# Cutting the last output tile in two and reordering the end-of-kernel waits in a fused attention-and-GEGLU kernel

## The chip, the cores and the metric

The kernel runs on one core of a Trainium2 chip (trn2). The metric is device time in microseconds (us), the median over runs of one kernel; a run's time is about 2 us longer than the span that its profile shows. The granted clock (the share of TensorE's full clock that its throttle let through) was 0.996 to 1.0. Engines in the profile: PE is TensorE's matmuls, PEld its weight loads, DVE is VectorE, ACT is ScalarE, POOL is GpSimd, SP is the sequencer that issues every DMA of this kernel ("SPq" is that sequencer).

## The reference

One normalised input feeds two branches, and both are added to the input. S is 2048 tokens, D is 512.

```python
xn = layernorm(x)                                   # [1, 2048, 512]
# A: 32 heads of 16, each token attends to 8 keys, at distances 0, 2, ..., 14
q, k, v = split(xn @ wqkv)
a = softmax(q . k[idx] * scale, masked where idx < 0) @ v[idx]
# B: GEGLU, hidden size 1376
h = gelu(xn @ w_gate) * (xn @ w_up)
out = x + a @ wo + h @ w_down
```

## The kernel before

The kernel is written as a graph of tasks (matmul groups, evictions, transfers). A list scheduler with a cost model orders them on each engine when the kernel is built; the chip then runs each engine's list in order, with semaphore waits where a task depends on another engine. The tokens are done in four blocks of 512. The last stage of a block makes four output tiles of 128 tokens: 11 matmuls with `Wd` (the down projection of B) and 4 with `Wo` (the output projection of A) accumulate in one bank of PSUM (the memory that matmuls write to), DVE adds the input rows `XR` and writes bf16 to `OB` (this is called the eviction of the bank), and SP stores `OB`:

```python
for ti in range(4):
    t = 4 * b + ti                       # t = 15 is the last tile of the kernel
    it_acc = Item("acc%d" % t, P_ps, "acc")
    it_ob = Item("ob%d" % t, P_ob, "ob") # two OB buffers
    # PE, task "acc": 11 x (HT_j x Wd_j), then 4 x (OT_dq x Wo_dq), all of 512 columns
    # DVE, task "fin":
    e.tensor_tensor(out=OB[:, ito.slot, :], in0=PS[:, 512*it.slot:512*it.slot+512],
                    in1=XR[:, itx.slot, :], op=ALU.add)
    # SP, task "sto":
    e.dma_start(out2[128*t:128*t+128, :], OB[:, it.slot, :])
    ...
```

Transfers rotate over 24 semaphores. When SP has issued the last transfer, the code lets it wait for the final value of each of them, in the order in which they were made:

```python
if eng_name == "sp":
    for (s, tot) in self.dma_totals:
        e.wait_ge(s, tot)
```

## Time and profile before

| | before |
|---|---|
| time, median of the first 3 runs | 214.04 us (213.99 to 214.37) |
| span in the profile | 212.0 us |
| PE busy | 203.9 us, 96% |
| end of the last matmul | 208.3 us |
| end of the last DVE instruction | 209.08 us |
| last store landed | 210.80 us |
| end of the span | 212.0 us |

From the page of the kernel before: the span, then each engine's busy time (share of the span, number of instructions), then the engines' shares of the chain that ended last. (26 records of matmuls are missing: the weight loads, one for each matmul, number 1548 here.)

```profile
span 212.0 us, 3824 instructions
PE 203.9 (96%) x1522; PEld 101.0 (48%) x1548; DVE 147.9 (70%) x237; ACT 115.2 (54%) x190; POOL 12.8 (6%) x44
PE 86%; DVE 7%; issue 2%; ACT 2%; DMA 1%; POOL 0%; ACTq 0%; DVEq 0%; POOLq 0%
```

The body of the kernel is one stream on PE. The end is not. These are lines of the timeline of the kernel before, for the last 8 us (start, duration, engine, line of the kernel, operation, what it writes and reads, count; in brackets the idle time before it and what ended that):

```profile
204.85 2.54 PE L1268 MATMUL PS<-Wd,HT 128*128 128x512 bf16 x11
205.87 3.57 SPq L1319 DMA_DIRECT2D out_dram<-OB  x2
207.23 1.03 PE L1281 MATMUL PS<-Wo,OT 128*128 128x512 bf16 x4
208.39 0.69 DVE L1313 TENSOR_TENSOR OB<-PS,XR 128x512 bf16<-128x512 f32 x1 [2.55 <-PE PS L1281]
```

The 15 matmuls of tile 15 start 0.216 us apart, the last at 207.88, and end at 208.26. The eviction runs from 208.39 to 209.08. The store is issued behind it (the second of the two that the SPq line merges, at 209.11). How long SP waited for the store is in the waits of the DMA queue (who waited for whom, total us, times, longest), and how long the store took from issue to landing is in the DMA view of the last 5 us (size, median us to landing):

```profile
SPq L512 <- DMA out_dram<-OB: 1.4, 1, 1.4
```

```profile
out_dram<-OB SPq DMA_DIRECT2D x1, 128.0 KB, 1.7
```

The line of the final waits itself, in the view of one source line (count, duration min/median/max in ns, first and last start in us), has its first record at 210.8, when the store has landed, and its last at 211.5:

```profile
L512 SPq EVENT_SEMAPHORE  x12: 17/28/28, 210.8 to 211.5; - x12
```

Which semaphores those records test is in the trace's raw records: start in us, duration in ns, engine, operation, `>=` for a semaphore it waits on. Semaphores 103 to 126 are the kernel's 24, in the order in which they were made, so 115 is place 12 of the list, counted from 0:

```
last landing of a transfer: 210.801
209.109 333 Sync DMA_DIRECT2D      $S[101]>= semaphore=115
210.817  17 Sync EVENT_SEMAPHORE   $S[115]>=
210.875  28 Sync EVENT_SEMAPHORE   $S[116]>= $S[114]>=
210.948  28 Sync EVENT_SEMAPHORE   $S[117]>= $S[113]>=
...
211.495  28 Sync EVENT_SEMAPHORE   $S[126]>= $S[104]>=
211.563  38 Sync COMPARE_BRANCH    $S[103]>=
```

So the 24 waits do not run as they are written. Place 12 runs first and alone, then pairs from the middle outward, and place 0 rides on the branch that leaves the block. The last store was the 133rd transfer, and that is place 12: the first wait blocked until the store had landed, and 0.76 us passed from there to the branch.

### The profile page before, as it was taken

What the parts mean: (1) busy time and instruction counts of PE and PEld (TensorE: products, weight loads), DVE (VectorE), ACT (ScalarE), POOL (GpSimd) and SP (SyncE); (2) the same over time, 40 slices, a digit from 0 to 9 for tenths busy, and PEclk for the clock granted to TensorE, in tenths of its full rate; (3) what the DMA queues carried; (4) which work ended last, traced back from release to release, by engine and by line L of the source; (5) the groups of instructions that cost most, each with busy time, mean ns of one, the idle gap of its engine ahead of it and who ended that gap; (6) DMA issues with size and microseconds to landing.
All of it is one profiled execution on the core that took longest, in us unless ns stands there. A gap on an engine that the chain in (4) does not pass through costs nothing.

```text
span 212.0 us, 3824 instructions
## 1 busy us (share of the span) xinstructions
PE 203.9 (96%) x1522; PEld 101.0 (48%) x1548; DVE 147.9 (70%) x237; ACT 115.2 (54%) x190; POOL 12.8 (6%) x44
## 2 busy tenths in 40 slices
PE   7999999999999999999999999999999999998993
PEld 2445565454444664544444654444445554443440
DVE  4508999999998597599822687697622877796121
ACT  2398667987810169976710259878400459847000
POOL 6701010010013000000000000000000000000000
PEclk9999999999999999999999999999999999999999
DMA  6999969023069610021011359030012258040111
GB/s 170 374 397 360 237 163 245 2 56 98 28 176 237 176 34 0 0 56 48 0 50 52 104 167 223 8 99 3 0 58 90 77 154 220 3 99 0 52 50 49
DMA packets 23489, 23.40 MB, mean 110 GB/s; under 512 B 2640, under 2 KB 22448, under 8 KB 23472
## 3 DMA queue, kind: packets, MB, share of 16 engines
q1 hardware_dynamic: 23472, 23.16, 38.6%
q8 instruction: 12, 0.20, 0.4%
q14 instruction: 5, 0.04, 0.1%
HBM read 18.94 MB, written 4.21 MB: 109 GB/s over the span
## 4 chain that ended last, share of the span: by engine, by line
PE 86%; DVE 7%; issue 2%; ACT 2%; DMA 1%; POOL 0%; ACTq 0%; DVEq 0%; POOLq 0%
PE PS L1229 31%; PE PS L1007 19%; PE PS L1268 18%; PE PS L1281 7%; PE PS L1069 6%; DVE PVS L1183 4%; PE PS L1198 3%; PE PS L965 2%; DVE st L894 1%; DMA XIN<-in_A_x_dram 1%; PE PS L1151 1%; DVE XN L952 1%; ACT PT L1160 1%; ACT xnT L973 0%; DVE HT L1250 0%
## 5 line engine op out<-in xcount | busy, mean ns | idle before, releaser
L1051 DVE TENSOR_TENSOR PROD<-QT,KT 128x2048 bf16<-128x2048 bf16 x32 | 37.3, 1219 | 11.5 <-ACT KT L1025 11.5
L1229 PE MATMUL PS<-xnT,Wu 128*128 128x512 bf16 (+1 forms) x171 | 44.4, 379 | 0.3
L1229 PE MATMUL PS<-xnT,Wg 128*128 128x512 bf16 (+1 forms) x171 | 44.2, 379 | 0.3
L1268 PE MATMUL PS<-Wd,HT 128*128 128x512 bf16 (+1 forms) x171 | 40.2, 379 | 0.4 <-ACT OT L1209 0.2
L1183 DVE TENSOR_TENSOR PVS<-BS,PT 128x2048 bf16<-128x2048 bf16 x32 | 37.0, 1219 | 3.6 <-ACT PT L1160 3.5
L1313 DVE TENSOR_TENSOR OB<-PS,XR 128x512 bf16<-128x512 f32 x16 | 11.0, 689 | 32.4 <-PE PS L1281 32.3
L1238 ACT ACTIVATE GG<-PS 128x512 bf16<-128x512 f32 (+1 forms) x44 | 26.6, 606 | 6.4 <-PE PS L1229 5.9
L1007 PE MATMUL PS<-xnT,Wqkv 128*128 128x512 bf16 x121 | 29.1, 379 | 1.0 <-issue 0.5
L1245 ACT ACTIVATE UU<-PS 128x512 bf16<-128x512 f32 (+1 forms) x44 | 26.6, 605 | 4.6 <-PE PS L1229 4.4
L1032 ACT ACTIVATE VT<-PS 128x512 bf16<-128x512 f32 x16 | 9.6, 598 | 34.4 <-PE PS L1007 34.4
L1268 PEld LDWEIGHTS PS<-Wd,HT 128*128 128x128 bf16 (+1 forms) x176 | 17.1, 98 | 21.0 <-ACT OT L1209 0.6
L1229 PEld LDWEIGHTS PS<-xnT,Wu 128*128 128x128 bf16 (+1 forms) x176 | 16.9, 100 | 18.6 <-ACT QT L1018 0.4
L1229 PEld LDWEIGHTS PS<-xnT,Wg 128*128 128x128 bf16 (+1 forms) x176 | 17.0, 100 | 18.1
L1025 ACT ACTIVATE KT<-PS 128x512 bf16<-128x512 f32 x16 | 9.6, 598 | 18.5 <-PE PS L1007 18.5
L1007 PEld LDWEIGHTS PS<-xnT,Wqkv 128*128 128x128 bf16 x128 | 11.9, 98 | 15.9 <-ACT KT L1025 0.8
L1250 DVE TENSOR_TENSOR HT<-GG,UU 128x512 bf16<-128x512 bf16 (+1 forms) x44 | 16.8, 419 | 2.2 <-ACT UU L1245 2.2
L1069 PEld LDWEIGHTS PS<-E,PROD 128*128 128x128 bf16 x512 | 15.8, 96 | 4.5
L1281 PE MATMUL PS<-Wo,OT 128*128 128x512 bf16 x64 | 16.4, 378 | 0.0
L1069 PE MATMUL PS<-E,PROD 128*128 128x8 bf16 x512 | 15.8, 166 | 0.0
L1007 PE MATMUL PS<-xnT,WV 128*128 128x512 bf16 x60 | 14.9, 378 | 0.3
L894 DVE BATCH_NORM_STATS2 st<-XIN 128x6 f32<-128x512 bf16 x16 | 10.7, 686 | 2.8 <-DMA XIN<-in_A_x_dram 2.8
L973 ACT ACTIVATE xnT<-PS 128x1024 bf16<-128x1024 bf16 x8 | 8.2, 1020 | 6.8 <-PE PS L965 6.8
(57 smaller groups left out, 148.4 us busy)
## 6 DMA issues: line engine op xcount, KB each, us to landing
BS<-vt_scratch SPq DMA_DIRECT2D x64, 128.5 KB, 3.4
XR<-in_A_x_dram SPq DMA_DIRECT2D x16, 128.0 KB, 2.2
vt_scratch<-VT SPq DMA_DIRECT2D x16, 128.0 KB, 1.7
out_dram<-OB SPq DMA_DIRECT2D x16, 128.0 KB, 2.0
XIN<-in_A_x_dram SPq DMA_DIRECT2D x7, 256.0 KB, 3.5
Wg<-in_B_w_gate_dram SPq DMA_DIRECT2D x1, 1376.0 KB, 9.2
Wu<-in_B_w_up_dram SPq DMA_DIRECT2D x1, 1376.0 KB, 12.2
Wd<-in_B_w_down_dram SPq DMA_DIRECT2D x1, 1280.0 KB, 10.3
```

The costliest lines, as they stand in the source:

```text
L894: return lambda e: e.bn_stats(out=st[:, t, :], in_=XIN[:, it.slot, t2, :])
L1007: ins = e.matmul(PS[:, 512 * it.slot:512 * it.slot + HWD], lhsT=lhsT, rhs=xnT[:, kt, c0:c0 + HWD], start=(kt == 0), stop=(kt == 3))
L1051: return lambda e: e.tensor_tensor(out=PROD[:, it.slot, :, :], in0=bass.AP(QT, (itq.slot * 4 + g) * 512, [[NQT * 4 * 512, 128], [0, 4], [1 ...
L1069: ins = e.matmul(PS[:, col:col + 8], lhsT=PROD[:, it.slot, jj, ti * 128:(ti + 1) * 128], rhs=E8[:, :], start=True, stop=True)
L1183: return lambda e: e.tensor_tensor(out=PVS[:, ito.slot, half, :, :], in0=BS[:, it.slot, :, o:o + 512], in1=bass.AP(PT, (itp.slot * 2 + hal ...
L1229: ins = e.matmul(PS[0:M, 512 * it.slot:512 * it.slot + 512], lhsT=Wx[:, kt, j * 128:j * 128 + M], rhs=xnT[:, kt, c0b:c0b + 512], start=(kt ...
L1238: return lambda e: e.activation(out=GG[0:M, ito.slot, :], in_=PS[0:M, 512 * it.slot:512 * it.slot + 512], func=ACTF.Gelu_apprx_tanh)
L1245: return lambda e: e.activation(out=UU[0:M, ito.slot, :], in_=PS[0:M, 512 * it.slot:512 * it.slot + 512], func=ACTF.Identity)
L1250: return lambda e: e.tensor_tensor(out=HT[0:M, ito.slot, j, :], in0=GG[0:M, ig.slot, :], in1=UU[0:M, iu.slot, :], op=ALU.mult)
L1268: ins = e.matmul(PS[:, 512 * it.slot:512 * it.slot + 512], lhsT=HT[0:K, ith.slot, j, ti * 128:(ti + 1) * 128], rhs=Wd[0:K, j, :], start=(j ...
L1281: ins = e.matmul(PS[:, 512 * it.slot:512 * it.slot + 512], lhsT=OT[:, ito.slot, dq, ti * 128:(ti + 1) * 128], rhs=Wo[:, dq, :], start=Fals ...
L1313: return lambda e: e.tensor_tensor(out=OB[:, ito.slot, :], in0=PS[:, 512 * it.slot:512 * it.slot + 512], in1=XR[:, itx.slot, :], op=ALU.add)
```

## The change

Its intent is to shorten what happens after the last matmul. It lists the final waits so that the oldest transfers are tested first and the newest on the branch, and it cuts tile 15 into 384 and 128 columns, each with its own PSUM bank, eviction, output buffer and store. It also generalises the loads of `Wg` and `Wu` to chunks, but the default is one chunk of all 11 column groups, which is the two loads of before.

```diff
         if eng_name == "sp":
-            for (s, tot) in self.dma_totals:
+            newest = {id(t.sem): i for i, t in enumerate(self.order["sp"])}
+            totals = sorted(self.dma_totals, key=lambda x: newest[id(x[0])])
+            n = len(totals)
+            runs_in = [n // 2]
+            for i in range(1, n // 2):
+                runs_in += [n // 2 + i, n // 2 - i]
+            runs_in.append(0)
+            listed = [None] * n
+            for place, x in zip(runs_in, totals):
+                listed[place] = x
+            for (s, tot) in listed:
                 e.wait_ge(s, tot)
...
+    TAIL_SPLIT = cfg.get("TAIL_SPLIT", [15])
...
-                it_acc = Item("acc%d" % t, P_ps, "acc")
-                it_ob = Item("ob%d" % t, P_ob, "ob")
+                cparts = [(0, 384), (384, 512)] if t in TAIL_SPLIT else [(0, 512)]
+                for ci, (c0, c1) in enumerate(cparts):
+                    CW = c1 - c0
+                    it_acc = Item("acc" + sfx, P_ps, "acc")
+                    it_ob = Item("ob" + sfx, P_ob, "ob")
...                  # matmuls with rhs Wd[0:K, j, c0:c1] and Wo[:, dq, c0:c1]
-                    G.task("dve", "fin%d" % t, 0.69, mk_fin(), rd=[it_acc, it_xr], wr=[it_ob], prio=base + 61)
+                        G.task("dve", "fin" + sfx, 0.16 + CW * 1.04e-3, mk_fin(), rd=[it_acc, it_xr], wr=[it_ob],
+                               prio=base + 61)
...
-                    return lambda e: e.dma_start(out2[128 * t:128 * t + 128, :], OB[:, it.slot, :])
+                        return lambda e: e.dma_start(out2[128 * t:128 * t + 128, c0:c1], OB[:, it.slot, 0:CW])
```

More of the change, by code (lines that the diff above doesn't have):

```diff
@@ L659, in bass_parallel_sum__sliding_local_dilated__glu_gated_geglu__prompt_kernel @@
     R_WD = cfg.get("R_WD", 100)
+    R_WG = cfg.get("R_WG", -800)
+    TAIL_SPLIT = cfg.get("TAIL_SPLIT", [15])
     NHALF = cfg.get("NHALF", [1, 1, 1, 1])
@@ L855, in bass_parallel_sum__sliding_local_dilated__glu_gated_geglu__prompt_kernel, with mk @@
                                       prio=13))
-        G.task("sp", "ld_wg", 0, lambda e: e.dma_start(
-            Wg[:, :, :], B_w_gate.rearrange("(k p) n -> p k n", p=128)), wr=[I_wg], prio=-800, nbytes=DF * 1024)
-        G.task("sp", "ld_wu", 0, lambda e: e.dma_start(
-            Wu[:, :, :], B_w_up.rearrange("(k p) n -> p k n", p=128)), wr=[I_wu], prio=-799, nbytes=DF * 1024)
+        WCH = cfg.get("WCHUNK", [11])
+        wch_of = {}
+        j0 = 0
+        for ci, nj in enumerate(WCH):
+            c_lo = j0 * 128
+            c_hi = min(DF, (j0 + nj) * 128)
+            for j in range(j0, j0 + nj):
+                wch_of[j] = ci
+            for (nm, Wx, I_w, src) in (("g", Wg, I_wg, B_w_gate), ("u", Wu, I_wu, B_w_up)):
+                def mk(Wx=Wx, src=src, c_lo=c_lo, c_hi=c_hi):
+                    return lambda e: e.dma_start(
+                        Wx[:, :, c_lo:c_hi], src[:, c_lo:c_hi].rearrange("(k p) n -> p k n", p=128))
+                G.task("sp", "ld_w%s%d" % (nm, ci), 0, mk(), wr=[(I_w, ci)], prio=R_WG + 2 * ci + (nm == "u"),
+                       nbytes=(c_hi - c_lo) * 1024)
+            j0 += nj
         G.task("sp", "ld_wd0", 0, lambda e: e.dma_start(
@@ L1234, in bass_parallel_sum__sliding_local_dilated__glu_gated_geglu__prompt_kernel @@
                     G.task("pe", "f%s%d_%d" % (nm, b, j), d_mm(512, 4), mk_f(),
-                           rd=[(I_xnT, 2 * b), (I_xnT, 2 * b + 1), I_w], wr=[it_p], prio=fb + j, mode="f")
+                           rd=[(I_xnT, 2 * b), (I_xnT, 2 * b + 1), (I_w, wch_of[j])], wr=[it_p], prio=fb + j,
+                           mode="f")
                 def mk_gl(it=it_g, ito=it_gg, M=M):
@@ L1256, in bass_parallel_sum__sliding_local_dilated__glu_gated_geglu__prompt_kernel @@
                 t = 4 * b + ti
-                it_acc = Item("acc%d" % t, P_ps, "acc")
                 it_xr = Item("xr%d" % t, P_xr, "xr")
-                it_ob = Item("ob%d" % t, P_ob, "ob")
-                fin_pe = FIN_PE or (t >= FIN_PE_FROM)
-                def mk_ad(ti=ti, it=it_acc, ith=it_ht, itx=it_xr, fin_pe=fin_pe):
-                    def f(e):
-                        ins = None
-                        for j in range(NJ):
-                            K = 128 if j < 10 else DF - 1280
-                            ins = e.matmul(PS[:, 512 * it.slot:512 * it.slot + 512],
-                                           lhsT=HT[0:K, ith.slot, j, ti * 128:(ti + 1) * 128], rhs=Wd[0:K, j, :],
-                                           start=(j == 0), stop=False)
-                        if fin_pe:
-                            ins = e.matmul(PS[:, 512 * it.slot:512 * it.slot + 512], lhsT=ident[:, :],
-                                           rhs=XR[:, itx.slot, :], start=False, stop=False)
-                        return ins
-                    return f
@@ L1277, in mk_aw @@
-                def mk_aw(ti=ti, it=it_acc, ito=it_ot):
-                    def f(e):
-                        ins = None
-                        for dq in range(4):
-                            ins = e.matmul(PS[:, 512 * it.slot:512 * it.slot + 512],
-                                           lhsT=OT[:, ito.slot, dq, ti * 128:(ti + 1) * 128], rhs=Wo[:, dq, :],
-                                           start=False, stop=(dq == 3))
-                        return ins
-                    return f
@@ L1286, in bass_parallel_sum__sliding_local_dilated__glu_gated_geglu__prompt_kernel @@
-                rd_d = [it_ht, I_wd] + ([it_xr, I_ident] if fin_pe else [])
-                if ACC_SPLIT:
-                    G.task("pe", "accd%d" % t, d_mm(512, 12 if fin_pe else 11), mk_ad(), rd=rd_d, wr=[it_acc],
-                           prio=base + R_ACCD, mode="f")
-                    G.task("pe", "accw%d" % t, d_mm(512, 4), mk_aw(), rd=[it_ot, I_wo, it_acc], wr=[it_acc],
-                           prio=base + 60, mode="f")
-                else:
-                    def mk_a(fd=mk_ad(), fw=mk_aw()):
-                        def f(e):
-                            fd(e)
-                            return fw(e)
-                        return f
-                    G.task("pe", "acc%d" % t, d_mm(512, 16 if fin_pe else 15), mk_a(),
-                           rd=rd_d + [it_ot, I_wo], wr=[it_acc], prio=base + 60, mode="f")
@@ L1303, in bass_parallel_sum__sliding_local_dilated__glu_gated_geglu__prompt_kernel @@
                 G.task("sp", "ldxr%d" % t, 0, mk_xr(), wr=[it_xr], prio=base + 58, nbytes=128 * 1024)
-                if fin_pe:
-                    def mk_fin(it=it_acc, ito=it_ob):
-                        return lambda e: e.activation(
-                            out=OB[:, ito.slot, :], in_=PS[:, 512 * it.slot:512 * it.slot + 512],
-                            func=ACTF.Identity)
-                    G.task("act", "fin%d" % t, d_act(512), mk_fin(), rd=[it_acc], wr=[it_ob], prio=base + 61)
-                else:
-                    def mk_fin(it=it_acc, itx=it_xr, ito=it_ob):
-                        return lambda e: e.tensor_tensor(
-                            out=OB[:, ito.slot, :], in0=PS[:, 512 * it.slot:512 * it.slot + 512],
-                            in1=XR[:, itx.slot, :], op=ALU.add)
-                    G.task("dve", "fin%d" % t, 0.69, mk_fin(), rd=[it_acc, it_xr], wr=[it_ob], prio=base + 61)
@@ L1318, in mk_so, with mk_ad, f, mk_aw @@
-                def mk_so(t=t, it=it_ob):
-                    return lambda e: e.dma_start(out2[128 * t:128 * t + 128, :], OB[:, it.slot, :])
-                G.task("sp", "sto%d" % t, 0, mk_so(), rd=[it_ob], wr=[(I_out, t)], prio=base + 62,
-                       nbytes=128 * 1024)
+                fin_pe = FIN_PE or (t >= FIN_PE_FROM)
+                cparts = [(0, 384), (384, 512)] if t in TAIL_SPLIT else [(0, 512)]
+                for ci, (c0, c1) in enumerate(cparts):
+                    CW = c1 - c0
+                    sfx = "%d" % t if len(cparts) == 1 else "%d_%d" % (t, ci)
+                    it_acc = Item("acc" + sfx, P_ps, "acc")
+                    it_ob = Item("ob" + sfx, P_ob, "ob")
+                    def mk_ad(ti=ti, it=it_acc, ith=it_ht, itx=it_xr, fin_pe=fin_pe, c0=c0, c1=c1, CW=CW):
+                        def f(e):
+                            ins = None
+                            for j in range(NJ):
+                                K = 128 if j < 10 else DF - 1280
+                                ins = e.matmul(PS[:, 512 * it.slot:512 * it.slot + CW],
+                                               lhsT=HT[0:K, ith.slot, j, ti * 128:(ti + 1) * 128],
+                                               rhs=Wd[0:K, j, c0:c1], start=(j == 0), stop=False)
+                            if fin_pe:
+                                ins = e.matmul(PS[:, 512 * it.slot:512 * it.slot + CW], lhsT=ident[:, :],
+                                               rhs=XR[:, itx.slot, c0:c1], start=False, stop=False)
+                            return ins
+                        return f
+                    def mk_aw(ti=ti, it=it_acc, ito=it_ot, c0=c0, c1=c1, CW=CW):
+                        def f(e):
+                            ins = None
+                            for dq in range(4):
+                                ins = e.matmul(PS[:, 512 * it.slot:512 * it.slot + CW],
+                                               lhsT=OT[:, ito.slot, dq, ti * 128:(ti + 1) * 128],
+                                               rhs=Wo[:, dq, c0:c1], start=False, stop=(dq == 3))
+                            return ins
+                        return f
+                    rd_d = [it_ht, I_wd] + ([it_xr, I_ident] if fin_pe else [])
+                    nmm = 12 if fin_pe else 11
+                    if ACC_SPLIT:
+                        G.task("pe", "accd" + sfx, d_mm(CW, nmm), mk_ad(), rd=rd_d, wr=[it_acc],
+                               prio=base + R_ACCD, mode="f", util=CW / (CW + 128.0))
+                        G.task("pe", "accw" + sfx, d_mm(CW, 4), mk_aw(), rd=[it_ot, I_wo, it_acc], wr=[it_acc],
+                               prio=base + 60, mode="f", util=CW / (CW + 128.0))
+                    else:
+                        def mk_a(fd=mk_ad(), fw=mk_aw()):
+                            def f(e):
+                                fd(e)
+                                return fw(e)
+                            return f
+                        G.task("pe", "acc" + sfx, d_mm(CW, nmm + 4), mk_a(),
+                               rd=rd_d + [it_ot, I_wo], wr=[it_acc], prio=base + 60, mode="f",
+                               util=CW / (CW + 128.0))
+                    if fin_pe:
+                        def mk_fin(it=it_acc, ito=it_ob, CW=CW):
+                            return lambda e: e.activation(
+                                out=OB[:, ito.slot, 0:CW], in_=PS[:, 512 * it.slot:512 * it.slot + CW],
+                                func=ACTF.Identity)
+                        G.task("act", "fin" + sfx, d_act(CW), mk_fin(), rd=[it_acc], wr=[it_ob], prio=base + 61)
+                    else:
+                        def mk_fin(it=it_acc, itx=it_xr, ito=it_ob, c0=c0, c1=c1, CW=CW):
+                            return lambda e: e.tensor_tensor(
+                                out=OB[:, ito.slot, 0:CW], in0=PS[:, 512 * it.slot:512 * it.slot + CW],
+                                in1=XR[:, itx.slot, c0:c1], op=ALU.add)
+                        G.task("dve", "fin" + sfx, 0.16 + CW * 1.04e-3, mk_fin(), rd=[it_acc, it_xr], wr=[it_ob],
+                               prio=base + 61)
+                    def mk_so(t=t, it=it_ob, c0=c0, c1=c1, CW=CW):
+                        return lambda e: e.dma_start(out2[128 * t:128 * t + 128, c0:c1], OB[:, it.slot, 0:CW])
+                    G.task("sp", "sto" + sfx, 0, mk_so(), rd=[it_ob], wr=[(I_out, (t, ci))], prio=base + 62,
+                           nbytes=128 * CW * 2)
```

## The prediction

> **What bounds the kernel now.** The page: span 212.0 us (timed 214.04), PE busy 203.9 us (96%), clock granted in full, DVE 70%, ACT 54%. The chain of waits is 86% PE: the body is a TensorE stream, and the diff adds and removes no matmul there. What it can touch is the end. From the timeline of the last microseconds (from the span's start): tile 15 is 15 matmuls of 512 columns, 0.216 us apart; the last ends at 208.27; the last DVE eviction runs 208.39 to 209.08 (0.69); the last store is issued at 209.11 (0.33); the waits show SP held 1.4 us by that store; then twelve end-of-kernel semaphore waits run from 210.8 to 211.5, 0.06 us apart; a barrier closes the span at 212.0. So 3.7 us pass after the last matmul.
>
> **What the change does.**
> 1. Order of the end waits. The records show that the 24 waits don't run as written: place 12 runs alone, then pairs (13,11), (14,10) ... (23,1), and place 0 rides on the closing branch. 133 DMAs over 24 semaphores put the last store on place 12, so the first wait blocks until the store has landed and the other eleven records run after it. The new list is made for this order: oldest first, newest on the branch. The eleven then run while the store is in flight. About -0.74 us (from 210.8 to the branch).
> 2. Tile 15 in 384+128 columns.
>  - PE: 15 matmuls of 384 (estimate 0.163 us each) plus 15 of 128. The eight-matmul transpose groups of 128 columns take 0.61 us with a last one of 0.22, so 0.056 us each, as the Trainium skill has it ("TensorE: Matmul & The Clock Gate", Part 1: 55.6 ns warm at N=128). 2.44+0.84 = 3.28 against 3.24: +0.04 us. The weight loads (97 ns) kept up in those groups.
>  - Last eviction: 128 instead of 512 columns. About 1.04 ns per column and 0.16 fixed: 0.29 for 0.69, -0.40 us. The 384-column part (0.56) is done before the last matmuls end.
>  - Last store: 32 KB in 256-byte rows for 128 KB in 1-KB rows. Its packets spread over 0.5 us (45 ns per 1-KB packet, eight per engine); with short ones I expect -0.2 us. The skill ("DMA: Bandwidth & Descriptors", Specifications) says that under 512 B a read-modify-write is done; no packet of 256 B is in this trace, so this term could vanish. The extra issue (0.35) fits in SP's idle time.
> 3. One weight chunk of 11 is the same two loads in the same order: 0.
> 4. The list scheduler's input changes by a hair (fin cost 0.690 to 0.692, numbering of the XR loads). The order in the body may flip somewhere: 0 +- 0.7 us.
>
> **Critical path.** All of 1 and 2 is on it: -0.74 +0.04 -0.40 -0.2 = -1.3 us. Prediction 212.75 us (-0.6%), range 211.9 to 213.7. Faster by over 2%: 0.02; within 2%: 0.96; slower by over 2%: 0.02.
>
> **What would show it.** The blocking wait is on the last record or the branch, nothing but the barrier (0.4-0.5 us) after the landing; the last DVE record is about 0.29 us at about 208.4; issue to landing of the last store is 1.5 us, not 1.7; matmuls of 128 columns 56 ns apart; tile 15's matmuls start near 204.9, as before.
>
> **What would make it wrong.** A different schedule in the body (tile 15 starts elsewhere than 204.9); 128-column matmuls held by weight loads (up to +0.6); the last store queued behind the 384-column one; the waits running in another order.

## The result

| | before | after |
|---|---|---|
| time, median (runs) | 214.03 us (14) | 212.71 us (11) |
| lowest to highest | 213.95 to 214.50 | 212.59 to 214.12 |

The difference of the medians is 1.32 us. The ratio is 0.9942, with a 95% interval of 0.9929 to 0.9955. A ratio here is the mean time of one kernel's runs over the mean of the other's runs of the same rounds, so it is not quite the ratio of the medians; the one run of 214.12 us is in it.

From the page of the kernel after, the same three lines:

```profile
span 211.0 us, 3857 instructions
PE 203.7 (97%) x1537; PEld 101.5 (48%) x1563; DVE 148.2 (70%) x238; ACT 115.2 (55%) x190; POOL 12.8 (6%) x44
PE 87%; DVE 6%; issue 2%; ACT 2%; DMA 1%; POOL 1%; ACTq 0%; SPq 0%; DVEq 0%; POOLq 0%
```

The timeline of the kernel after, for its last 8 us:

```profile
205.24 1.95 PE L1299 MATMUL PS<-Wd,HT 128*128 128x384 bf16 x11
207.03 0.81 PE L1312 MATMUL PS<-Wo,OT 128*128 128x384 bf16 x4
207.68 0.78 PE L1299 MATMUL PS<-Wd,HT 128*128 128x128 bf16 x11
207.98 0.56 DVE L1342 TENSOR_TENSOR OB<-PS,XR 128x384 bf16<-128x384 f32 x1 [1.75 <-PE PS L1312]
208.30 0.39 PE L1312 MATMUL PS<-Wo,OT 128*128 128x128 bf16 x4
208.79 0.29 DVE L1342 TENSOR_TENSOR OB<-PS,XR 128x128 bf16<-128x128 f32 x1 [0.26 <-PE PS L1312]
```

Two things are to be seen. The larger eviction (0.56) now runs while PE still works on the smaller part, and only 0.29 us of eviction is left after the last matmul, for 0.69. And tile 15 starts at 205.24, which is 0.39 later than in the profile of before. That is no part of the change. In these first lines of each timeline the statistics of the first two input tiles run at 2.85 as one stretch in the kernel before, while in this profile of the kernel after, DVE sat idle for 0.33 us before the second tile, whose load landed at 3.81 instead of 3.36:

```profile
2.85 1.29 DVE L894 BATCH_NORM_STATS2 st<-XIN 128x6 f32<-128x512 bf16 x2 [2.85 <-DMA XIN<-in_A_x_dram]
```

```profile
2.82 0.69 DVE L917 BATCH_NORM_STATS2 st<-XIN 128x6 f32<-128x512 bf16 x1 [2.82 <-DMA XIN<-in_A_x_dram]
3.84 0.69 DVE L917 BATCH_NORM_STATS2 st<-XIN 128x6 f32<-128x512 bf16 x1 [0.33 <-DMA XIN<-in_A_x_dram]
```

That load was issued at 1.22 in both, and in nine of the ten other runs it landed at 3.30 to 3.40. Comparing the two traces instruction by instruction, DVE and ACT are 0.38 to 0.39 us later from 8 us until tile 15's evictions. The order of tasks on every engine is also the same in both kernels but for tile 15. So the body is untouched, and the time before tile 15 varies from run to run: in the profiles tile 15 starts anywhere from 204.83 to 205.44 in kernels whose bodies are the same. (At 205.44, in the run on one buffer, it was not the head: against the run of the cut alone DVE fell 0.5 us behind between 25 and 31 us. Why, is not known.) Read the tail from tile 15's first matmul, therefore, not from the span's start. The waits of the queue, the line of the final waits, and the last two stores, after:

```profile
SPq L686 <- DMA out_dram<-OB: 0.4, 1, 0.4
```

```profile
L522 SPq EVENT_SEMAPHORE  x12: 17/28/28, 209.5 to 210.2; - x12
```

```profile
out_dram<-OB SPq DMA_DIRECT2D x1, 96.0 KB, 1.6
out_dram<-OB SPq DMA_DIRECT2D x1, 32.0 KB, 1.4
```

All twelve records are now done at 210.2, before the store has landed (210.55), and the wait for the store is at the branch (L686 is the end of the block). The raw records say the same; the last store is now the 134th transfer, on semaphore 116:

```
209.109 332 Sync DMA_DIRECT2D      $S[101]>= semaphore=116
209.493  17 Sync EVENT_SEMAPHORE   $S[117]>=
...
210.171  28 Sync EVENT_SEMAPHORE   $S[114]>= $S[115]>=
last landing of a transfer: 210.553
210.568  38 Sync COMPARE_BRANCH    $S[116]>=
```

The accounts of both traces, counted from tile 15's first matmul, in us:

| step | before | after | difference |
|---|---|---|---|
| last matmul ends (modelled) | 3.405 | 3.446 | +0.041 |
| from there to the last eviction's start | 0.136 | 0.108 | -0.028 |
| last eviction | 0.691 | 0.292 | -0.399 |
| from its end to the last store's issue | 0.026 | 0.026 | 0 |
| issue to landing | 1.692 | 1.444 | -0.248 |
| landing to the branch | 0.762 | 0.015 | -0.747 |
| branch to the end of the span | 0.389 | 0.390 | 0 |
| sum | 7.101 | 5.721 | -1.380 |

### The profile page after: what moved, and what is told of

Read it like the earlier page. It is cut to its first block, busy times and chain, and to the rows that moved or that the text cites. A ratio compares the mean times of both kernels' runs of the same rounds, so it can differ in the third digit from the quotient of the medians.

```text
span 211.0 us, 3857 instructions
## 1 busy us (share of the span) xinstructions
PE 203.7 (97%) x1537; PEld 101.5 (48%) x1563; DVE 148.2 (70%) x238; ACT 115.2 (55%) x190; POOL 12.8 (6%) x44
## 4 chain that ended last, share of the span: by engine, by line
PE 87%; DVE 6%; issue 2%; ACT 2%; DMA 1%; POOL 1%; ACTq 0%; SPq 0%; DVEq 0%; POOLq 0%
PE PS L1252 31%; PE PS L1030 20%; PE PS L1299 18%; PE PS L1312 7%; PE PS L1092 6%; DVE PVS L1206 4%; PE PS L1221 3%; PE PS L988 2%; DMA XIN<-in_A_x_dram 1%; PE PS L1174 1%; POOL sq L932 1%; DVE st L917 1%; DVE XN L975 1%; ACT PT L1183 1%; ACT xnT L996 0%
## 5 line engine op out<-in xcount | busy, mean ns | idle before, releaser
L1299 PE MATMUL PS<-Wd,HT 128*128 128x512 bf16 (+3 forms) x182 | 40.4, 367 | 0.4 <-ACT OT L1232 0.2
L1342 DVE TENSOR_TENSOR OB<-PS,XR 128x512 bf16<-128x512 f32 (+2 forms) x17 | 11.2, 658 | 31.8 <-PE PS L1312 31.8
L1299 PEld LDWEIGHTS PS<-Wd,HT 128*128 128x128 bf16 (+1 forms) x187 | 17.8, 98 | 20.6 <-ACT OT L1232 0.6
L1312 PE MATMUL PS<-Wo,OT 128*128 128x512 bf16 (+2 forms) x68 | 16.6, 365 | 0.0
```

The costliest lines, as they stand in the source:

```text
L1299: ins = e.matmul(PS[:, 512 * it.slot:512 * it.slot + CW], lhsT=HT[0:K, ith.slot, j, ti * 128:(ti + 1) * 128], rhs=Wd[0:K, j, c0:c1], start ...
L1312: ins = e.matmul(PS[:, 512 * it.slot:512 * it.slot + CW], lhsT=OT[:, ito.slot, dq, ti * 128:(ti + 1) * 128], rhs=Wo[:, dq, c0:c1], start=F ...
L1342: return lambda e: e.tensor_tensor(out=OB[:, ito.slot, 0:CW], in0=PS[:, 512 * it.slot:512 * it.slot + CW], in1=XR[:, itx.slot, c0:c1], op= ...
```

## The experiments

The theory: the gain is the sum of independent savings behind the last matmul, of which the waits give 0.75 us and the cut 0.63 us. The rivals: one of the two gives it all; or the cut helps by freeing buffers, wherever it stands; or the store's size doesn't matter; or short rows carry a penalty of their own. Each kernel computed a correct result. In all of them the order of tasks is that of the kernel after, save for what the experiment edits.

### The waits alone

The kernel before, with the new order of waits (the first hunk of the change) and an uncut tile 15.

> The kernel before with the new order of the end waits alone. Theory (two independent savings after the last matmul: waits 0.74-0.75 us, tile split 0.63-0.64 us): 0.75 us faster than before, 213.28 us, ratio 0.9965. In the trace the last store's landing is followed by the branch within 0.03 us instead of 0.76. Rival 1 (the waits are idle bookkeeping, the whole gain is the split): ratio 1.000. Rival 2 (all of the gain is the waits): ratio 0.994.

Measured: 213.34 us (213.22 to 213.57, 5 runs) against 214.06; ratio 0.9964 (0.9952 to 0.9975). In its trace the landing is followed by the branch after 0.017 us, for 0.762 before; the last eviction (0.692) and the issue to landing (1.697) are as before. The theory holds and rivals 1 and 2 both fall.

### The cut alone

```diff
-            for (s, tot) in listed:        # and the lines that make the list
+            for (s, tot) in self.dma_totals:
```

> The changed kernel with the end waits in the order they were made. There are now 134 stores and loads, so the last one is on place 13, which the second record tests, not the first; ten pairs and the branch follow it, about 0.68 us. Theory: split saves 0.64 us and one record (0.06) less waits after the landing: 0.70 us faster than before, 213.33 us, ratio 0.9967. Rival 2 (gain all in the waits): 1.000. Rival 1 (gain all in the split): 0.994. The savings of this run and of the waits-only run should add up to that of the whole change within 0.1 us, less the 0.06 counted twice.

Measured: 213.32 us (213.29 to 213.85, 5 runs); ratio 0.9966 (0.9954 to 0.9979). The waits of the DMA queue in this kernel show the blocking waits at the first two records (L512), which the two parts' stores hold in turn:

```profile
SPq L512 <- DMA out_dram<-OB: 1.1, 2, 0.7
```

The second record, on the last store's semaphore, passes at 210.21, and the branch runs at 210.90, 0.704 us after the landing. The medians of the two halves save 0.72 and 0.74 us; together 1.46, less the 0.06 that both count, makes 1.40, which is near the 1.32 of the medians and the 1.38 of the traces. The halves add up.

### A plain sort instead of the middle-out list

```diff
-            ... (runs_in, listed)
+            for (s, tot) in sorted(self.dma_totals, key=lambda x: newest[id(x[0])]):
```

> The changed kernel with the waits simply sorted, oldest first, newest last as written. Theory (waits run middle first, then outward in pairs, place 0 on the branch): the newest stands on place 23 and is tested in the last record before the branch, so only that record's end and the branch follow the landing: 0.06 us slower than the change, 212.8 us, ratio 0.9945. Rival (waits run as written): the wait on the newest is the very last, same as the change to the last 0.01 us; and then the change's own list, newest at place 0, would have blocked first. The trace must show which semaphore the branch waits on: here the oldest-but-many one that passes at once, while the record before it blocks.

Measured: 212.74 us (212.68 to 213.77, 6 runs); ratio 0.9943. The times can't tell this from the change, but the records can:

```
last landing of a transfer: 210.227
210.243  28 Sync EVENT_SEMAPHORE   $S[116]>= $S[118]>=
210.311  38 Sync COMPARE_BRANCH    $S[117]>=
```

The newest semaphore (116), written last, is tested in the last record before the branch, and the branch waits on 117, which was written first. The landing is followed by the branch after 0.084 us, for 0.015 with the change's list. So the middle-out order is real, and a plain sort gets all but 0.07 us of the saving.

### Two evictions, one store

Both parts are evicted into the two column ranges of one output buffer, and one transfer stores it.

```diff
-                    it_ob = Item("ob" + sfx, P_ob, "ob")
+                    if ci == 0:
+                        it_ob = Item("ob%d" % t, P_ob, "ob")
-   out=OB[:, ito.slot, 0:CW]        (eviction)
+   out=OB[:, ito.slot, c0:c1]
-   G.task("sp", "sto" + sfx, ...)   (one store for each part)
+   if ci == len(cparts) - 1: G.task("sp", "sto%d" % t, ...)   (rows of 1 KB, 128 KB)
```

> The changed kernel with tile 15 still evicted in 384 and 128 columns but into one buffer, stored by one 128 KB transfer of 1-KB rows. It takes the short store away and keeps the short eviction. Theory (eviction 0.40, store 0.25): 0.25 us slower than the change, about 212.95 us, ratio to before 0.9953; the last store's issue to landing is 1.69 us as in the kernel before, the last eviction 0.29. Rival (the store's cost is fixed latency, its size doesn't matter): as fast as the change, 0.994.

Measured: 213.22 us, but spread from 212.73 to 213.36 over 6 runs; ratio 0.9952 (0.9940 to 0.9964). The spread is wider than the step in question, so the verdict is the trace's: issue to landing is 1.688 us, as in the kernel before, and the eviction is 0.292. The size of the store is worth 0.25 us and the rival falls. (By the ratio alone it would not: its interval just reaches the rival's 0.994.) What neither theory had is that the last eviction starts 3.483 us after tile 15's first matmul, 0.07 sooner than in the change, so that the tail is 0.175 longer than the change's and not 0.25. The run on one buffer, below, tests why.

### Other cuts: 256 and 448 columns

```diff
-cparts = [(0, 384), (384, 512)]
+cparts = [(0, 256), (256, 512)]      # and, in a second kernel, [(0, 448), (448, 512)]
```

> The changed kernel with tile 15 cut at 256 instead of 384: last part 256 columns, last store 64 KB in 512-byte rows. Theory (fixed plus per-column costs, no penalty for short rows): TensorE time unchanged, last eviction 0.43 us (+0.14), last store 0.07 longer: 0.2 us slower than the change, 212.9 us, ratio 0.9952. Rival (a read-modify-write punishes rows under 512 B): the 512-byte rows save on the store, its issue to landing is shorter than the change's 1.44, and the kernel is as fast as the change.

> The changed kernel cut at 448: last part 64 columns, 128-byte rows. Theory: the smaller part no longer decides; the 448-column eviction (0.63 us) outlasts the 64-column matmuls (15 x 0.029 = 0.44), the second eviction (0.23) queues behind it on DVE, and the second store queues behind the first one's issue on the sequencer: last issue about 0.25 us later than the change's, landing 0.06 sooner after it: 0.2 us slower than the change, 212.9 us. Rival (the narrower the last part the better): 0.1 us faster than the change, 212.6 us.

Measured: 212.88 us for 256 (212.85 to 213.47, 5 runs; ratio 0.9947, 0.9934 to 0.9959) and 213.04 us for 448 (212.93 to 213.12, 5 runs; ratio 0.9948, 0.9936 to 0.9960). Both intervals contain the change's 0.9942, so the ratios can't rank the three cuts; the traces can. Lines of the timeline of the kernel cut at 256, then of that cut at 448:

```profile
207.75 0.60 PE L1312 MATMUL PS<-Wo,OT 128*128 128x256 bf16 x4
208.46 0.43 DVE L1342 TENSOR_TENSOR OB<-PS,XR 128x256 bf16<-128x256 f32 x1 [1.19 <-PE PS L1312]
```

```profile
208.09 0.76 DVE L1342 TENSOR_TENSOR OB<-PS,XR 128x448 bf16<-128x448 f32 x2 [2.15 <-PE PS L1312]
208.11 0.28 PE L1312 MATMUL PS<-Wo,OT 128*128 128x64 bf16 x4
```

Cut at 256, DVE idles 1.19 us between its two evictions and the last one is longer than it need be. Cut at 448, the two evictions run back to back (x2, no idle time between them): matmuls of 64 columns are 0.029 us apart, the 15 of them are done before the 0.625 us eviction ahead is, and the last eviction starts 3.683 us after tile 15's first matmul, for 3.554 in the change. The last store is issued at 4.170, for 3.872. Its issue to landing was expected to be 0.06 shorter and was 0.08 longer (1.522 for 1.444): it is issued 0.38 us behind the store of 112 KB, and its first packet starts 0.94 us after its issue, for 0.83 in the change, just behind the larger one's packets. (Its issue itself took 0.431 us, for 0.332 in the change, which is about the same difference; whether that or the packets ahead held it back is not shown.) The cut at 384 stands near the balance of the two evictions. From tile 15's first matmul to the end the three cuts take 5.947 (256), 5.721 (384) and 6.097 (448).

The packets of these stores, and of the one in 1-KB rows, give the cost of a row in this direction (median time of one packet on its DMA engine):

| row | 128 B | 256 B | 512 B | 768 B | 1024 B |
|---|---|---|---|---|---|
| packet | 13 ns | 18 ns | 27 ns | 36 ns | 46 ns |

That is 8.5 ns plus 0.036 ns for each byte to within 0.7 ns throughout. A short row does cost more for each byte (0.070 ns at 256 B, 0.045 at 1024 B), because of the fixed part. But there is no step at 512 B, and the 512-byte rows did not land sooner (1.534). The rival that rows under 512 B carry a penalty of their own falls, for these stores.

### The cut in the last tile but one

```diff
-    TAIL_SPLIT = cfg.get("TAIL_SPLIT", [15])
+    TAIL_SPLIT = cfg.get("TAIL_SPLIT", [14])
```

> The changed kernel with tile 14 cut instead of tile 15. Theory (the split pays only because nothing computes after it): all of the split's saving is lost and the 0.04 us of TensorE time stays, so it is the waits-only kernel plus 0.04: 213.35 us, ratio 0.9967. Rival (narrower evictions or stores help wherever they stand, by freeing buffers sooner): as fast as the change, 0.994.

Measured: 213.33 us (213.27 to 213.37, 5 runs); ratio 0.9961 (0.9947 to 0.9975), as the waits alone (213.34). The last eviction is 0.691 and the store's issue to landing 1.689, as before. A narrow part that has other work behind it gains nothing.

### One buffer, two stores

The edit of "Two evictions, one store", but each part is stored by itself as soon as it is evicted (`OB[:, it.slot, c0:c1]`).

> The changed kernel with both parts of tile 15 evicted into one output buffer (its two column ranges), still stored by two transfers. In the change the second eviction takes the buffer that tile 14's store was read from, so it has a second semaphore to test: its record of 21 ns stands ahead of it and the eviction starts 0.108 us after the last matmul's modelled end; in the run with one store, which had no such wait, 0.037. Theory (one more wait record costs 0.07 us even when it passes at once): in the trace the last eviction starts 3.483 us after tile 15's first matmul instead of 3.554, and all else is as in the change; 0.07 us faster, 212.64 us, less than the rounds can tell. Rival (the single store, not the wait, made the eviction start sooner): 3.554 as in the change.

Measured: 212.66 us (212.56 to 213.10, 5 runs); ratio 0.9933 (0.9918 to 0.9949). By time it can't be told from the change. In the trace the last eviction starts 3.484 after tile 15's first matmul, for 3.554, and the tail is 5.660 for 5.721. The records of DVE at the last eviction show the difference; the kernel before, the kernel after, then this one:

```
208.297  50 Vector EVENT_SEMAPHORE  $S[99]>= $S[112]>=
208.392 691 Vector TENSOR_TENSOR    $S[113]>= $S[101]++
```

```
208.725  21 Vector EVENT_SEMAPHORE  $S[99]>=
208.791 292 Vector TENSOR_TENSOR    $S[114]>= $S[101]++
```

```
208.921 293 Vector TENSOR_TENSOR    $S[99]>= $S[101]++
```

In the change the second eviction takes the buffer that tile 14 was stored from, so it must test that store's semaphore (114) beside PE's (99). With two conditions one stands in a record of its own ahead of the eviction. Here that is PE's, the one that comes last, so the record can't pass early. The Trainium skill ("Perfetto Trace Analysis", Identifying Dependency Chains) says that instructions waiting on several engines may have such records inserted ahead of them; this trace agrees, and shows that it costs 0.07 us on the critical path although tile 14's store had landed at 207.96, 0.83 us before the eviction. In the kernel before, the last eviction tests three semaphores (PE's, the load of `XR`, the store of tile 13) and its record takes 50 ns. From the last matmul's end to the eviction it is thus 0.136 us with three conditions, 0.108 with two and 0.037 with one.

### A candidate: work for the gap before the last four tiles

The tail was the part of the kernel where PE waits. The experiments showed that each stretch without computing there counts in full, and the trace of both kernels has one more such stretch. Lines of the timeline of the kernel after, before its last four tiles:

```profile
190.61 2.36 DVE L1206 TENSOR_TENSOR PVS<-BS,PT 128x2048 bf16<-128x2048 bf16 x2
192.88 1.43 DVE L1274 TENSOR_TENSOR HT<-GG,UU 128x512 bf16<-128x512 bf16 x4
193.11 1.05 PE L1221 MATMUL PS<-PVS,E 128*32 128x512 bf16 x16 [0.44 <-ACT UU L1269]
194.09 1.25 PE L1372 MATMUL PS<-wsrc 128*128 128x512 bf16 x5
194.37 1.08 ACT L1232 ACTIVATE OT<-PS 128x512 bf16<-128x512 f32 x2
195.50 0.82 PE L1299 MATMUL PS<-Wd,HT 128*128 128x512 bf16 x3 [0.16 <-ACT OT L1232]
```

PE waits 0.44 (in the end for ACT's eviction of `UU`, at 193.07; the last products of the attention, `PVS`, were ready at 192.97), does a reduction of the attention, runs five filler matmuls (`wsrc`, whose results nobody reads), and waits until 195.50 for the last eviction of OT. But tile 12's first eleven matmuls don't read OT; they wait because all 15 are one task. The edit makes two tasks of the first ten: six ahead of the reduction, four behind it.

```diff
+    EARLY = [(0, 6), (6, 10)]        # parts of tile 12's matmuls with Wd
...
+for pi, (ja, jb) in enumerate(EARLY if t == 12 else []):
+    G.task("pe", "accp%d_%d" % (t, pi), d_mm(512, jb - ja), mk_p(),   # matmuls j = ja .. jb-1
+           rd=[(it_ht, j) for j in range(ja, jb)] + [(I_wd, 0)], wr=[it_acc], prio=..., mode="f")
+    # the first part is ordered after the last w_up matmuls; the rest of tile 12 starts at j = 10
```

> A candidate that may beat both. In both kernels TensorE has a gap before the last four tiles: 0.44 us at 192.7 (waiting for the last products of the attention), then 1.25 us of filler matmuls and 0.16 us idle until 195.50, waiting for the last OT eviction, though tile 12's first eleven matmuls need only HT. Here six of them run before the last attention reduction and four after it, and only the eleventh and the four with Wo wait for OT. Theory (the end is a TensorE stream behind that gap): tile 12 ends 1.5 to 1.7 us sooner, and the whole kernel is 1.5 us faster than the change, about 211.1 us, ratio 0.9865. Rival (the gap only hides other work that ends last): 0 to 0.4 us.

Measured: 211.39 us (211.37 to 211.47, 4 runs); ratio 0.9872 (0.9858 to 0.9885). It beats both kernels: 2.67 us under the kernel before of the same rounds, and 1.32 under the median of the change. Lines of its timeline:

```profile
190.30 2.35 DVE L1208 TENSOR_TENSOR PVS<-BS,PT 128x2048 bf16<-128x2048 bf16 x2
192.46 1.46 PE L1332 MATMUL PS<-Wd,HT 128*128 128x512 bf16 x6
193.84 1.05 PE L1223 MATMUL PS<-PVS,E 128*32 128x512 bf16 x16
194.82 1.04 PE L1332 MATMUL PS<-Wd,HT 128*128 128x512 bf16 x4
194.94 1.09 ACT L1234 ACTIVATE OT<-PS 128x512 bf16<-128x512 f32 x2 [0.79 <-PE PS L1223]
196.09 0.39 PE L1301 MATMUL PS<-Wd,HT 96*128 96x512 bf16 x1 [0.22 <-ACT OT L1234]
```

The fillers are gone (the scheduler no longer finds a gap that is long enough). Counted from the last pair of products of the attention on DVE (190.61 in the kernel after, 190.30 in this one), tile 15 starts after 14.63 us there (at 205.24) and 13.36 here (at 203.66), 1.27 sooner. Ten matmuls, 2.16 us, no longer stand behind OT; but with six of them ahead of it the reduction runs later, and OT is ready 0.89 later on the same count (at 196.03, for 195.45). PE waits for it again (0.22 in brackets, behind the four matmuls), and this is about what the expected 1.5 had left out. The rest of the 1.32 is within what the start of tile 15 varies by.

### Both together

> Both improvements together: tile 12's first ten matmuls moved into the gap, and one output buffer for the two parts of tile 15. Theory: they add, since one ends before the other begins: 211.39 - 0.07 = 211.32 us, ratio to before 0.9869. Rival: no further change, 211.39.

Measured: 211.55 us (211.40 to 211.93, 4 runs); ratio 0.9880 (0.9861 to 0.9900). In the trace the tail is 5.662, for 5.722 in the candidate alone, so the 0.06 us is there. The times don't show it: the runs of this kernel scatter over 0.5 us, and its median is 0.16 above the candidate's. The candidate is the fastest kernel by measured time; whether the one buffer makes it faster can't be told by these rounds.

## Why the prediction was right

The time lay in the range: predicted 212.75, measured 212.71. Point by point, with the trace's numbers:

- **The waits, predicted -0.74.** Measured -0.747 in the two traces, and 0.72 by the medians when done alone. The step that carried it was to read the order from the trace's records instead of from the code.
- **PE's time, predicted +0.04.** Measured +0.041. The matmuls of 128 columns are 55 to 56 ns apart (two are 58 and 60), as the transposes of that width in the trace of before were, and as the Trainium skill has it ("TensorE: Matmul & The Clock Gate", Part 1). Those of 384 are 0.161 to 0.166 apart, for the estimate of 0.163.
- **The last eviction, predicted 0.29 for 0.69.** Measured 0.292 for 0.691.
- **The last store, predicted -0.2.** Measured -0.248; this term was sized a little too small. The doubt that rows under 512 B might cost it did not come true.
- **Not in the prediction:** the last eviction starts 0.028 sooner after the matmuls than before, with two semaphores to test for three. The prediction also missed what the second output buffer adds to it, a wait record of 0.07 us; without that the change would have been 0.06 to 0.07 better.
- **The schedule of the body, predicted 0 +- 0.7.** It did not change: the task order is the same on each engine, and the two traces run 0.38 to 0.39 apart throughout. What looks like a miss, tile 15 at 205.24 instead of 204.9, is the later landing of one input tile in that run (3.81 instead of 3.36).

The sum of the parts in the traces, -1.38, agrees with -1.32 by the medians and with the predicted -1.3. The two terms that were off (0.048 of the store, 0.028 before the eviction) have the same sign, so the sum is not right by cancelling.

## What to carry to other kernels

In this kernel what stands behind the last matmul counted in full, however small: make the last piece of work narrow enough that the eviction before it has just finished, and no narrower, and do this only to the piece that has nothing behind it. Put the wait on the newest transfer where it runs last, and check in the trace's records in which order the waits really run. Then look for the other places where the busiest engine waits for an operand that only the end of a task needs; splitting that task was worth about as much here as the whole change.

## What the Trainium skill lacked or had wrong

- No page of it tells in what order a long list of final waits runs, or what each costs. Here 24 waits became a first record with the middle one, eleven pairs outward, and the branch with place 0, about 0.06 us apart on SP (0.76 us from the landing to the branch).
- "DMA: Bandwidth & Descriptors", Specifications, gives 512 B as the smallest transfer for line rate, with a read-modify-write below it. The stores show no step there: 13, 18, 27, 36 and 46 ns for packets of 128, 256, 512, 768 and 1024 B, a line of 8.5 ns plus 0.036 ns per byte.
- "Perfetto Trace Analysis", Identifying Dependency Chains, says that wait records may be inserted, without a cost. Here one on DVE, made because the eviction had two semaphores to test, cost 0.07 us on the critical path although the second of them had been met 0.83 us before.
- "DMA: Bandwidth & Descriptors", Anatomy of one DMA, gives a fit of about 2.0 us fixed plus the bytes, for transfers issued by GpSimd, and none for stores issued by SP. These took 1.69 us for 128 KB and 1.44 for 32 KB here, which is 1.36 us fixed by a line through these two; the 64 KB store's 1.53 lies on it.
